# One table of steps in a new order: 31 stretches of 64-row products for 39 in a retention-and-MLP kernel

## The chip, the core and the metric

The kernel runs on one core of a Trainium2 chip. The metric is the device time of one launch in microseconds (us). Five engines work side by side, each through its own queue in order: TensorE (PE, with its weight loads shown as PEld), VectorE (DVE), ScalarE (ACT), GpSimd (POOL) and SyncE (SP), which here only issues transfers.

## What is computed

```python
# q, k, v: (8, 8, 576, 64) = batch, head, position, width; w_in 512x2048, w_out 2048x512
scores = scale * q @ k.T                      # per batch and head
ret    = scores * Dmat                        # Dmat[h, i, j] = gamma[h] ** (i - j) for i >= j, else 0
attn   = ret @ v
x = attn.transpose(0, 2, 1, 3).reshape(4608, 512)
h = x @ w_in
s = sin(alpha * h)
g = h + s * s / (alpha + 1e-9)
out = g @ w_out                               # float32
```

## The kernel before

The work is cut into nine blocks of 512 tokens: blocks 0 to 7 are the first 512 positions of one batch each, block 8 gathers the last 64 positions of all eight. Blocks pass through one pipeline: while the projections of block n run, the attention of block n+1 and the output product of block n-1 are woven in between.

*Attention.* Each batch is done in two parts p of 256 positions. `scores b p y` makes the scores of half the heads with 64x64 pieces of the PE array (16 products, line 1564), `masked` multiplies them by the decay mask on DVE (line 1576), `outer` adds up the key-value state (64-row products, line 1506), `values b p False` and `values b p True` multiply the masked scores with v (line 1606), and `add_states` adds the state of the earlier positions (line 1628); `keep` copies the result into the block's x. The state goes through `more` (two POOL operations) and `to_state`. `load` brings raw q, k and v, `cast` scales and halves them to 16 bits, and `crossed` turns them by a transfer.

*MLP.* Each of a block's 16 units is: `project` (four products of 128 rows and 512 columns, line 1745, into a PSUM bank), `sine` on ACT (line 1753), `square` on an engine that the step names (line 1762 on ACT, line 1764 on DVE or POOL), and `product` on DVE (line 1769), which writes gT and frees the bank. For blocks 0 to 2 the second matrix product is `gemm2` (four products, line 1785). Blocks 3 to 8 use a Strassen scheme instead: `weight_sum` and `row_sum` (line 1832; S1 to S4 of gT, in two parts) and seven `part_product`s of 16 products each (line 1849), read out by `after_product`.

*Order.* Everything is issued by hand from a table of 1,214 steps. A step's words say what is done, on which engine (A is ACT, V is DVE, G is POOL) and at which buffer (`@...`) or PSUM bank (op, h0, h1, h2, and m0 and m1, which are two banks each). A step issues its instructions at the end of their engines' queues. So the table alone sets each queue's order, and semaphores do the rest.

Two details matter. The two halves of `values` write the same bank by different row halves of the array. In blocks 0 to 3 PE runs dry between them:

```python
def change_rows(key):
    if key in open_turns:
        nc.tensor.drain()
        open_turns.clear()
```

`values False` puts its key into `open_turns`, and `values True` calls `change_rows`; one call empties the list for both parts. In blocks 4 to 7 `values ... False relay=G` places a mark (an empty instruction) in POOL's queue instead, and `values True` of that part waits for the mark.

Of the kernel before, what the change touches and what calls it, by code (L numbers as in the profile page):

```python
# [210 lines left out]
load 2 v 0 @raw5
load 3 k 0 @raw1
wait_for_w_out 1
load 2 v 1 @raw0
cast 2 v 1 G @v160
at.values 1 0 False m1
at.values 1 0 True
at.add_states 1 0
at.keep 1 0 V @xT1
at.next_sum 1 3  # L220
crossed 2 1 k @kT0
cast 2 v 0 G @v161
at.to_state 1 3 G
cast 2 k 0 V @k162
crossed 2 1 q @qT0
crossed 2 0 k @kT1
crossed 2 0 q @qT1
load 4 q 1 @raw2
load 3 v 0 @raw4
load 3 v 1 @raw0  # L230
load 4 v 0 @raw5
load 3 q 1 @raw3
finish 0 1
at.to_state 1 2 A
finish 0 3
at.values 1 1 True
at.add_states 1 1
gemm2 0 1 h0
gemm2 0 2 h0
at.keep 1 1 A  # L240
project 1 7 m1
project 1 6 m0
gemm2 0 3 h0
sine 1 7 @s3
# [30 lines left out]
sine 1 14 @s0  # L275
at.outer 2 (0,1) m1
at.scores 2 1 1 m0
at.evict 2 (0,1) A @kvs0
at.to_state 2 0 G @s160
cast 3 k 0 G @k163  # L280
at.more 2 1 @s321
at.more 2 2 @s320
at.to_state 2 2 G
at.more 2 3 @s321
at.to_state 2 3 G
at.to_state 2 1 G
product 1 5
gemm2 0 8 h0
gemm2 0 9 h0
square 1 9 V @ss3  # L290
product 1 9
at.masked 2 1 1 @ret0
square 1 14 A @ss0
product 1 14
sine 1 1 @s2
square 1 1 A @ss2
product 1 1
project 1 0 m1
at.scores 2 0 0 m0
project 1 4 h2  # L300
project 1 3 h1
project 1 2 op
at.masked 2 0 0 @ret1
sine 1 0 @s1
square 1 0 A @ss1
sine 1 4 @s3
square 1 4 A @ss3
sine 1 3 @s0
square 1 3 A @ss0
product 1 0  # L310
product 1 3
product 1 4
load 4 v 1 @raw1
sine 1 2 @s2
at.scores 2 0 1 m0
at.scores 2 1 0 m1
gemm2 0 10 h0
gemm2 0 11 h0
project 1 15 h1
project 1 12 h2  # L320
square 1 2 A @ss2
product 1 2
finish 0 2
gemm2 1 4 h0
gemm2 1 5 h0
at.masked 2 1 0 @ret2
sine 1 15 @s1
at.masked 2 0 1 @ret3
at.values 2 1 False m1
at.values 2 0 False m0  # L330
at.values 2 0 True
at.add_states 2 0
sine 1 12 @s3
square 1 12 V @ss1
product 1 12
cast 3 v 0 A (0) @v162
cast 3 v 0 V (1)
cast 3 v 1 A @v163
at.values 2 1 True
at.add_states 2 1  # L340
at.outer 3 (0,1) op h2
at.evict_bank 3 1 A @kvs0
at.evict_bank 3 0 A
at.more 3 1 @s320
square 1 15 V @ss0
load 4 k 0 @raw4
# [29 lines left out]
at.to_state 3 1 A
project 2 7 h2
sine 2 7 @s0
square 2 7 A @ss3
project 2 2 h0  # L380
crossed 3 0 q @qT2
project 2 1 m0
project 2 6 m1
project 2 3 op
finish 1 3
project 2 0 h1
sine 2 1 @s2
sine 2 2 @s3
square 2 2 A @ss2
product 2 7  # L390
gemm2 1 0 h2
product 2 2
# [3 lines left out]
sine 2 3 @s1
sine 2 6 @s0
square 2 1 A @ss1
product 2 1
at.scores 3 1 1 m0  # L400
square 2 6 A @ss0
sine 2 0 @s3
square 2 0 A @ss3
# [24 lines left out]
at.scores 3 0 1 m1
at.masked 3 0 1 @ret0
cast 4 k 1 G @k162  # L430
at.outer 4 (0,1) op h0
square 2 13 G @ss3
at.evict_bank 4 0 A @kvs0
at.scores 3 0 0 m0
at.masked 3 0 0 @ret2
project 2 14 h2
at.evict_bank 4 1 V
product 2 13
at.to_state 4 0 A @s160
at.more 4 1 @s321  # L440
project 2 8 op
at.values 3 1 False m1
# [47 lines left out]
load 0 v 2  # L490
load 1 v 2
make_mask_halved
project 3 0 h0
sine 3 0 @s3
square 3 0 A @ss2
weight_sum T3 0 V
product 3 0
gemm2 2 0 op
cast 5 v 0 G @v162
cast 5 k 1 G @k160  # L500
load 0 k 2
load 1 k 2
cast 5 q 1 G @q161
project 3 1 h1
sine 3 1 @s2
project 3 2 h2
sine 3 2 @s0
# [24 lines left out]
product 3 1
cast 5 v 1 G @v163
square 3 6 A @ss0
gemm2 2 6 op
project 3 7 h1
at.scores 4 1 0 m1
sine 3 7 @s1
product 3 6
cast 0 v 2 G  # L540
at.masked 4 1 0 @ret1
square 3 7 A @ss1
# [1488 lines left out]
```

## Time and profile before

| | us |
|---|---|
| median of three runs | 298.53 |
| lowest and highest | 297.3 and 298.81 |
| the profiled execution, whole | 297.56 |
| its span, first to last instruction | 295.8 |
| busy in it: PE, DVE, ACT, POOL | 284.9, 223.8, 218.1, 141.0 |
| DMA: moved, mean rate | 49.95 MB, 169 GB/s |

PE is the longest queue by 60 us. A row of the chain of waits names the start, the length and the work that ended last there; the same row as "PE ... x16" means that PE's own queue was the last thing waited for. Busy times of PE are modelled from starts, so small gaps are better read from the chain.

### The profile page before, as it was taken

To read this page: it belongs to the slowest core of one execution; us is meant where nothing else is said; L and a number is where in the kernel's file an instruction comes from. 1 tells how busy PE (TensorE), PEld (TensorE's weight loads), DVE (VectorE), ACT (ScalarE), POOL (GpSimd) and SP (SyncE) were. 2 spreads that over 40 slices of the span, in tenths; PEclk is the share of its full clock that TensorE was granted. 3 is DMA by queue.
4 is the path that set the end of the run, shared out by engine and by line. 5 is a ranking of instruction groups with operands and counts; after the bars stand their busy time and mean duration, and the time that the engine had idled before them with its cause. 6 is when DMAs were issued, how large, how long until landed. Compare 5 with 4: busy or idle time off the path is not lost.

```text
span 295.8 us, 8407 instructions
## 1 busy us (share of the span) xinstructions
PE 284.9 (96%) x3480; PEld 182.6 (62%) x3480; DVE 223.8 (76%) x316; ACT 218.1 (74%) x361; POOL 141.0 (48%) x151
## 2 busy tenths in 40 slices
PE   6789999999999999999999999999999999999993
PEld 4566545555545544455666666666776677676883
DVE  2596977788349776889988798869868785877863
ACT  2578935997595897977878896798679878888500
POOL 5684678565688685736439933956232000000000
PEclk9999999999999999999999999999999999999999
DMA  7999999998998999978899985984423101200124
GB/s 216 347 234 210 243 282 320 253 256 217 244 225 184 174 164 229 250 148 204 164 239 163 251 180 145 232 151 120 88 77 104 38 2 38 73 15 23 53 73 124
DMA packets 121767, 49.95 MB, mean 169 GB/s; under 512 B 78721, under 2 KB 119681, under 8 KB 121729
## 3 DMA queue, kind: packets, MB, share of 16 engines
q1 hardware_dynamic: 117920, 44.78, 63.5%
q0 software_dynamic: 2688, 4.19, 7.8%
q8 instruction: 27, 0.44, 0.6%
q10 hardware_dynamic: 1120, 0.44, 0.6%
q14 instruction: 12, 0.09, 0.1%
HBM read 36.75 MB, written 9.44 MB: 156 GB/s over the span
## 4 chain that ended last, share of the span: by engine, by line
PE 82%; DMA 9%; DVE 3%; ACT 2%; POOL 1%; SPq 1%; issue 1%; ACTq 0%; POOLq 0%
PE hps L1745 40%; PE hps L1849 23%; PE ops L1785 12%; DMA raw<-in_v_dram 3%; DMA w_in<-in_moe_w_in_dram 3%; PE o L1606 3%; PE sc L1564 2%; DMA raw<-in_k_dram 2%; DVE S L1832 1%; PE kv L1506 1%; DVE gT L1769 1%; PE o L1628 1%; SPq L1350 1%; POOL k L1396 1%; ACT s L1753 1%
## 5 line engine op out<-in xcount | busy, mean ns | idle before, releaser
L1769 DVE SCALAR_TENSOR_TENSOR gT<-ss,inva,hps 128x512 f16<-128x512 f16 x144 | 103.7, 743 | 36.0 <-ACT ss L1762 32.5
L1745 PE MATMUL hps<-xT,w_in 128*128 128x512 f16 (+1 forms) x532 | 120.2, 372 | 0.6 <-DMA w_in<-in_moe_w_in_dram 0.6
L1753 ACT ACTIVATE s<-hps,alpha_t 128x512 f16<-128x512 f32 x144 | 96.1, 683 | 30.4 <-PE hps L1745 29.5
L1745 PEld LDWEIGHTS <-w_in 128*128 128x128 f16 x596 | 65.6, 114 | 51.4 <-DMA w_in<-in_moe_w_in_dram 0.9
L1762 ACT ACTIVATE ss<-s 128x512 f16<-128x512 f16 x125 | 76.9, 629 | 5.9 <-DVE gT L1769 3.3
L1785 PE MATMUL ops<-w_out,gT 128*128 128x512 f16 x192 | 46.0, 380 | 0.0
L1849 PEld LDWEIGHTS <-gT 128*128 128x128 f16 x384 | 37.3, 98 | 7.5
L1396 POOL TENSOR_TENSOR k<-raw,cn 128x1024 f16<-128x1024 f32 (+1 forms) x17 | 29.5, 1736 | 20.9 <-DMA raw<-in_k_dram 18.4
L1849 PEld LDWEIGHTS <-S 128*128 128x128 f16 x288 | 28.1, 98 | 6.1
L1785 PEld LDWEIGHTS <-gT 128*128 128x128 f16 x192 | 17.9, 98 | 20.3
L1396 POOL TENSOR_TENSOR q<-raw,cn 128x1024 f16<-128x1024 f32 x13 | 25.1, 1937 | 3.7 <-PE o L1606 2.4
L1849 PE MATMUL hps<-T,gT 128*128 128x256 f16 x192 | 22.8, 273 | 0.0
L1849 PE MATMUL hps<-w_out,S 128*128 128x256 f16 x192 | 22.8, 273 | 0.0
L1849 PE MATMUL hps<-w_out,gT 128*128 128x256 f16 x192 | 22.8, 273 | 0.0
L1551 POOL TENSOR_TENSOR s<-kvs,cn 128x256 f32<-128x256 f32 x21 | 13.8, 659 | 16.3 <-ACT kvs L1320 8.8
L1322 POOL CAST v<-raw 128x1024 f16<-128x1024 f32 x10 | 10.3, 1037 | 21.8 <-DMA raw<-in_v_dram 20.0
L1576 DVE TENSOR_TENSOR ret<-sc,mask 128x1024 f16<-128x1024 f32 x16 | 19.2, 1219 | 1.6 <-PE sc L1564 1.6
L1552 POOL TENSOR_TENSOR kvs<-s,kvs 128x256 f32<-128x256 f32 x21 | 17.5, 833 | 3.9 <-DVE kvs L1322 1.2
L1576 DVE TENSOR_TENSOR ret<-sc,mask_halved 128x768 f16<-128x768 f32 x16 | 15.1, 954 | 3.7 <-PE sc L1564 3.6
L1320 ACT CAST xT<-o 128x1024 f16<-128x1024 f32 (+1 forms) x15 | 16.2, 1122 | 1.9 <-PE o L1628 1.9
L1832 DVE TENSOR_TENSOR S<-gT,S 128x1024 f16<-128x1024 f16 x24 | 17.4, 730 | 0.1
L1745 PE MATMUL hps<-xS,w_in 128*128 128x512 f16 x64 | 14.8, 379 | 0.0
(78 smaller groups left out, 265.6 us busy)
## 6 DMA issues: line engine op xcount, KB each, us to landing
raw<-in_q_dram SPq DMA_DIRECT2D x16, 512.0 KB, 5.3
out_dram<-osb SPq DMA_DIRECT2D x32, 256.0 KB, 2.9
raw<-in_k_dram SPq DMA_DIRECT2D x8, 512.0 KB, 6.1
raw<-in_v_dram SPq DMA_DIRECT2D x8, 512.0 KB, 6.3
raw<-in_v_dram SPq DMA_DIRECT2D x32, 128.0 KB, 3.5
raw<-in_k_dram SPq DMA_DIRECT2D x32, 128.0 KB, 3.7
w_in<-in_moe_w_in_dram POOLq DMA_DIRECT2D x4, 512.0 KB, 11.9
w_out<-in_moe_w_out_dram POOLq DMA_DIRECT2D x4, 512.0 KB, 13.2
```

What stands on the lines that cost most here:

```text
L1320: eng.copy(d_, s_)
L1396: eng.tensor_tensor(dst[:, a0:a1].rearrange("p a r t d -> p t (a r) d"), t_.rearrange("p (t a) x -> p t a x", t=2)[:, :, a0:a1].rearrange( ...
L1551: nc.gpsimd.tensor_tensor(s32, self.kvs[:, c - 1], g1.unsqueeze(2).to_broadcast([P, 4, D]), MULT)
L1552: nc.gpsimd.tensor_tensor(self.kvs[:, c], s32, self.kvs[:, c], ADD)
L1576: nc.vector.tensor_tensor(ret.rearrange("p t (z x) -> p (t z) x", z=2)[:, :, 0:n], sc.rearrange("p t (z x) -> p (t z) x", z=2)[:, :, 0:n], ...
L1745: matmul(hps_of[n, fc][0][:, cols], w_in16[fc // 4][:, a, fc % 4 :: 4], xs[n][:, a, cols], start=(a == 0 and part != 1), stop=(a == KT - 1 ...
L1753: nc.scalar.activation(s_t, hps, mybir.ActivationFunctionType.Sin, bias=0.0, scale=alpha_t[:, fc : fc + 1],)
L1762: nc.scalar.activation(ss_t, s_t, mybir.ActivationFunctionType.Square)
L1769: nc.vector.scalar_tensor_tensor(gT[n][:, fc, :], ss_t, inva[:, fc : fc + 1], hps, MULT, ADD)
L1785: matmul(ops[n, c, cols.start][:, cols], gT[n][:, fk, c * P : (c + 1) * P], w_out16[:, fk, cols], start=(fk == 0), stop=(fk == FC - 1), sk ...
L1832: made = eng.tensor_tensor(out_, x, y, op)
L1849: matmul(acc[:, 256 * j : 256 * j + 256], lhs[:, x, 128 * j : 128 * j + 128], rhs[:, x], start=(tag is not None and j == js[0] and p == 0 ...
```

## The change

The table keeps its 1,214 steps and every function; the multiset of matrix products, transfers and results is the same. From row 133 on, in block 0's last units, nearly every step has another place, and some have another engine, bank or buffer. A stretch is a run of 64-row products with no 128-row product between; there are 39 before and 31 after. Counted over the whole table, squares go from 125 on ACT, 11 on DVE and 8 on POOL to 84, 43 and 17; row sums from 48 on DVE to 28 on DVE and 20 on POOL; casts of q and k from 38 on POOL and 6 on DVE to 29 and 15; casts of v from 14 on POOL, 6 on ACT and 1 on DVE to 9, 10 and 2. Two lines of the difference:

```diff
-row_sum 4 S3 0 V
+row_sum 4 S3 0 G
...
-square 7 0 A @ss1
+square 7 0 V @ss1
```

PE, at block 4's first scores. `sc` is the PSUM tile of one `scores` step, `kT` and `qT` the turned keys and queries, `ops` a `gemm2` result. Before:

```order
L1564 MATMUL sc_2116<-qT0_205,kT1_259 64x64
L1564 LDWEIGHTS kT1_259
L1564 MATMUL sc_2116<-qT0_205,kT1_259 64x64
L1785 LDWEIGHTS gT_1584
L1785 MATMUL ops_2135<-w_out16_74,gT_1584 128x512
```

After, at the same block's first scores:

```order
L1564 MATMUL sc_2123<-qT2_344,kT1_259 64x64
L1564 LDWEIGHTS kT1_259
L1564 MATMUL sc_2123<-qT2_344,kT1_259 64x64
L1564 LDWEIGHTS kT3_1211
L1564 MATMUL sc_2140<-qT1_271,kT3_1211 64x128
```

A second group of 16 now follows the first at once, where a `gemm2` unit stood.

POOL, around the marks of block 5's `values`. The marks are empty and have no row: before, the second one stands between the rows of `vs16` and `q162`; after, both stand between the rows of `gT_2516` and `s320`. `vs16`, `k163` and `q162` are casts, `ss2` is a square, `gT_2516` a row sum, `kvs0` the state. Before:

```order
L1544 TENSOR_TENSOR s160_279<-kvs0_246,cn_67 128x256
L1544 TENSOR_TENSOR sS_75<-kvs0_246,cn_67 128x256 [waits Pool_49]
L1322 CAST vs16_2899<-vs32_2277 128x512
L1396 TENSOR_TENSOR q162_287<-raw1_123,cn_67 128x2x8x64 [waits PE_49]
L1551 TENSOR_TENSOR s321_776<-kvs0_246,cn_67 128x256 [waits Activation_49]
```

After:

```order
L1396 TENSOR_TENSOR k163_894<-raw0_121,cn_67 128x2x8x64 [waits DMAHW5_49,DMAHW6_49,DMAHW4_49,PE_49]
L1764 TENSOR_TENSOR ss2_541<-s1_523 128x512 [waits DVE_49,Activation_49]
L1396 TENSOR_TENSOR q162_287<-raw1_123,cn_67 128x2x8x64
L1832 TENSOR_TENSOR gT_2516<-gT_2516 128x4x256 [waits PE_49]
L1551 TENSOR_TENSOR s320_623<-kvs0_246,cn_67 128x256 [waits PE_49,Activation_49]
```

Ahead of the marks POOL now has two casts of 128x1024, a square and a row sum; before, two state operations and a small cast stood there.

DVE, in the second half of block 7. `gT` rows of line 1769 are `product`s, `S` and `gT<-gT` rows of line 1832 are row sums, `osb` a result. Before:

```order
L1769 SCALAR_TENSOR_TENSOR gT_4110<-ss2_541,inva_69,hps_4537 128x512
L1895 TENSOR_TENSOR osb_4595<-hps_4578,low_4157 128x512
L1769 SCALAR_TENSOR_TENSOR gT_4598<-ss1_539,inva_69,hps_4599 128x512
L1832 TENSOR_TENSOR gT_4110<-gT_4110 128x4x256
L1832 TENSOR_TENSOR S2_1_2582<-gT_4110 128x1024
L1832 TENSOR_TENSOR S1_1_2606<-gT_4110,S2_1_2582 128x1024
L1832 TENSOR_TENSOR S4_1_2776<-gT_4110,S2_1_2582 128x1024
```

After:

```order
L1769 SCALAR_TENSOR_TENSOR gT_4104<-ss1_539,inva_69,hps_4550 128x512
L1769 SCALAR_TENSOR_TENSOR gT_4104<-ss3_563,inva_69,hps_4557 128x512
L1769 SCALAR_TENSOR_TENSOR gT_4104<-ss1_539,inva_69,hps_4569 128x512
L1764 TENSOR_TENSOR ss0_525<-s2_537 128x512
L1895 TENSOR_TENSOR osb_4611<-hps_4586,low_4168 128x512
L1764 TENSOR_TENSOR ss3_563<-s3_550 128x512
L1832 TENSOR_TENSOR gT_4104<-gT_4104 128x4x256
```

Squares have come into DVE's queue, and of the four row sums of the second part one is left there.

More of the change, by code (lines that the diff above doesn't have):

```diff
@@ L218 @@
+cast 2 q 1 V @q160
+at.add_states 1 1
 at.add_states 1 0
 at.keep 1 0 V @xT1
-at.next_sum 1 3
-crossed 2 1 k @kT0
-cast 2 v 0 G @v161
[L223 to L244, printed above, removed]
@@ L272 @@
+square 1 7 V @ss2
+product 1 7
+cast 2 v 0 G @v161
+product 1 10
+square 1 5 G @ss1
+product 1 5
 sine 1 9 @s3
@@ L280 @@
+sine 1 0 @s2
+product 1 1
+project 1 3 h1
+load 3 v 0 @raw2
+sine 1 3 @s1
+square 1 3 A @ss0
+product 1 9
+load 3 v 1 @raw3
+load 4 v 0 @raw5
+square 1 0 A @ss2
+project 1 2 op
 cast 3 k 0 G @k163
-at.more 2 1 @s321
-at.more 2 2 @s320
+at.scores 2 0 0 m0
+gemm2 0 10 h0
+at.masked 2 0 0 @ret1
 at.to_state 2 2 G
[L284 to L309, printed above, removed]
 product 1 0
 product 1 3
-product 1 4
[L313 to L323, printed above, removed]
+sine 1 2 @s3
+square 1 2 A @ss3
@@ L324 @@
+cast 3 v 0 G (0) @v162
+project 1 4 h2
+sine 1 4 @s2
+square 1 4 A @ss2
+product 1 2
+gemm2 0 11 h0
+finish 0 2
+at.scores 2 1 0 m1
+at.scores 2 0 1 m0
+at.masked 2 0 1 @ret3
+project 1 15 h1
+load 3 q 0 @raw4
+load 0 v 2
+product 1 4
+project 1 12 op
+sine 1 12 @s1
+square 1 12 A @ss3
 gemm2 1 4 h0
+cast 3 v 1 A @v163
+at.masked 2 1 0 @ret2
+product 1 12
 gemm2 1 5 h0
-at.masked 2 1 0 @ret2
-sine 1 15 @s1
-at.masked 2 0 1 @ret3
+at.to_state 2 1 G
 at.values 2 1 False m1
+at.values 2 1 True
 at.values 2 0 False m0
@@ L331 @@
 at.values 2 0 True
-at.add_states 2 0
[L333 to L339, printed above, removed]
+cast 3 v 0 G (1)
+load 3 q 1 @raw3
+sine 1 15 @s2
+square 1 15 A @ss0
+at.outer 3 (0,1) op h2
+at.to_state 2 3 V
+at.add_states 2 0
 at.add_states 2 1
-at.outer 3 (0,1) op h2
+load 4 v 1 @raw0
+product 1 15
+cast 4 q 1 G @q160
 at.evict_bank 3 1 A @kvs0
[L343 to L346, printed above, removed]
@@ L376 @@
[L376 to L392, printed above, removed]
+load 4 k 0 @raw2
+cast 4 k 0 G (0) @k163
+sine 2 3 @s3
+product 2 6
 gemm2 1 8 h0
 gemm2 1 9 h0
-gemm2 1 10 h0
[L396 to L403, printed above, removed]
@@ L424 @@
-square 2 9 A @ss0
-product 2 9
-sine 2 13 @s3
 finish 1 0
+at.scores 3 0 0 m0
+load 5 q 1 @raw2
+load 1 v 2
+product 2 13
+at.masked 3 0 0 @ret2
 at.scores 3 0 1 m1
 at.masked 3 0 1 @ret0
[L430 to L435, printed above, removed]
-project 2 14 h2
[L437 to L442, printed above, removed]
+load 0 k 2
+at.outer 4 (0,1) h0 h1
+at.evict_bank 4 0 V @kvs0
@@ L490 @@
[L490 to L507, printed above, removed]
+project 3 2 h2
+sine 3 2 @s2
+square 3 0 V @ss0
+product 3 0
+project 3 1 h1
+sine 3 1 @s1
+project 3 4 m1
+sine 3 4 @s0
+product 2 12
+load 5 k 1 @raw4
+square 3 1 G @ss1
+cast 5 k 0 V @k162
+at.more 4 3 @s321
+square 3 2 A @ss3
@@ L532 @@
[L532 to L542, printed above, removed]
+crossed 5 0 k @kT2
+project 3 6 h2
+cast 0 v 2 G
+project 3 9 h0
+load 5 v 1 @raw5
+product 3 1
+at.scores 4 0 0 m0
+at.scores 4 1 0 m1
+sine 3 6 @s2
+gemm2 2 4 op
+load 6 v 0 @raw2
+project 3 7 h1
+at.to_state 4 3 G
+load 5 q 0 @raw0
+square 3 6 A @ss3
+gemm2 2 5 op
+at.masked 4 1 0 @ret1
+product 3 6
+load 3 v 2
@@ L576 @@
+sine 3 10 @s2
+square 3 10 V @ss2
+weight_sum T2 0 V
+at.to_state 4 2 A
 cast 0 k 2 G
+gemm2 2 8 op
 gemm2 2 9 op
 gemm2 2 10 op
-sine 3 12 @s0
-square 3 12 A @ss1
-product 3 12
-at.values 4 1 False m1 relay=G
-square 3 8 A @ss3
+gemm2 2 11 op
+product 3 10
+square 3 11 A @ss3
+product 3 11
+sine 3 8 @s2
+cast 5 q 0 V @q162
+at.values 4 0 False m0 relay=G
+finish 2 2
+at.values 4 1 False m1 relay=G
+cast 0 q 2 G
+at.outer 5 (0,1) h0 h2
+at.values 4 0 True
+at.values 4 1 True
+load 2 k 2
+square 3 8 A @ss0
@@ L706 @@
-square 4 10 A @ss1
-part_product 3 5 op
+product 3 14
+gemm2 2 15 op
+weight_sum T1 0 V
+project 4 5 h1
+square 3 13 A @ss2
+sine 4 2 @s3
+product 3 13
+at.more 5 2 @s321
+square 4 2 A @ss1
+cast 2 v 2 G
+product 4 0
+sine 4 5 @s2
+part_product 3 1 op
+project 4 7 m1
+weight_sum T4 0 V
+finish 2 3
+square 4 5 A @ss2
+cast 6 v 0 A @v160
+product 4 2
+product 4 5
+at.more 5 3 @s321
+at.scores 5 0 1 m0
+sine 4 7 @s3
+load 6 k 0 @raw4
+weight_sum T1 1 V
+row_sum 3 S2 1 V
+cast 6 k 0 G @k161
+project 4 1 h0
@@ new lines @@
+square 4 7 A @ss1
+weight_sum T2 1 V
+after_product 3 1
+project 4 3 h2
+part_product 3 2 - first=1
+product 4 7
+at.masked 5 0 1 @ret2
+load 6 q 1 @raw2
+at.scores 5 1 0 m1
+at.to_state 5 1 V
+sine 4 3 @s0
+square 4 3 A @ss2
+at.scores 5 0 0 m0
+row_sum 3 S1 1 V
+after_product 3 2
+project 4 4 h1
+row_sum 3 S4 1 V told_to=G
+at.masked 5 0 0 @ret3
+product 4 3
+sine 4 4 @s2
+part_product 3 6 op
+after_product 3 6
+at.masked 5 1 0 @ret1
+load 6 v 1 @raw4
+project 4 9 m0
+sine 4 1 @s3
+square 4 1 A @ss3
@@ new lines @@
+project 4 6 h2
+at.to_state 5 3
+square 4 4 A @ss2
+product 4 4
+product 4 1
+sine 4 9 @s0
+square 4 9 A @ss1
+product 4 9
+sine 4 6 @s0
+square 4 6 A @ss2
+product 4 6
+part_product 3 7 - first=6
+row_sum 3 S1 0 V
+project 4 10 h1
+at.to_state 5 2 G
+after_product 3 7
+project 4 8 h0
+load 3 k 2
+project 4 12 h2
+part_product 3 5 op
+at.scores 5 1 1 m0
+load 2 q 2
+load 3 q 2
+weight_sum T4 1 V
+cast 6 k 1 G @k163
+load 7 v 1 @raw0
+sine 4 10 @s1
+crossed 6 0 k @kT2
+sine 4 12 @s3
+cast 6 v 1 A @v161
@@ L774 @@
-square 5 1 A @ss1
-product 4 15
-project 5 2 m0
-sine 5 2 @s1
-project 5 6 h0
-square 5 2 A @ss3
+cast 2 k 2 V
+load 4 k 2
+crossed 2 2 k
+at.evict_bank 6 0 A @kvs0
+after_product 3 3
+square 4 11 V @ss2
+at.evict_bank 6 1 V
+at.more 6 1 @s320
+load 7 k 0 @raw1
+crossed 6 0 q @qT2
+product 4 11
+at.keep 5 0 A @xT0
+at.values 5 1 True
+at.add_states 5 1
+at.keep 5 1 A
+project 4 14 op
+sine 4 14 @s2
+row_sum 4 S2 0 V
+row_sum 4 S4 0 G
+at.more 6 2 @s321
+row_sum 4 S1 0 G
+square 4 14 A @ss3
+product 4 14
@@ new lines @@
+part_product 3 4 h0
+after_product 3 4
+project 4 13 h2
+sine 4 13 @s1
+at.more 6 3 @s320
+project 5 2 m1
+at.to_state 6 0 @s160
+project 5 0 m0
+load 5 k 2
+crossed 6 1 k @kT3
+project 4 15 h0
+cast 6 q 1 V @q160
+crossed 6 1 q @qT3
+part_product 4 1 op
+sine 5 0 @s3
+load 7 v 0 @raw2
+square 5 0 V @ss1
+square 4 13 A @ss0
+product 4 13
+product 5 0
+load 4 v 2
+load 5 v 2
+cast 7 v 0 G @v162
+project 5 3 h1
+sine 4 15 @s3
+square 4 15 A @ss2
+product 4 15
+after_product 4 1
+row_sum 4 S3 1 V
@@ L807 @@
+product 5 9
+at.scores 6 1 1 m0
+product 5 6
+square 5 4 A @ss0
+part_product 4 7 - first=6
+project 5 12 h1
+sine 5 12 @s2
+at.masked 6 1 0 @ret1
+row_sum 5 S3 0 G
+project 5 8 h0
+product 5 4
+after_product 4 7
+at.to_state 6 3
+row_sum 4 S1 1 V
+at.to_state 6 1
+project 5 7 h2
+project 5 5 m1
+part_product 4 5 op
+at.masked 6 1 1 @ret3
+sine 5 8 @s0
+square 5 8 A @ss3
+sine 5 7 @s0
+cast 7 q 0 G @q160
+square 5 12 A @ss2
+load 7 k 1 @raw1
+product 5 8
 cast 7 k 1 G @k163
-square 5 4 A @ss3
-product 5 4
@@ new lines @@
+crossed 4 2 k
+after_product 5 1
+part_product 5 2 - first=1
+row_sum 5 S2 1 V
+project 6 4 h1
+at.more 7 1 @s320
+at.masked 7 0 1 @ret2
+at.scores 7 1 0 m0
+square 6 1 G @ss2
+crossed 2 2 q
+product 6 1
+at.scores 7 1 1 m1
+after_product 5 2
+sine 6 4 @s2
+sine 6 2 @s1
+row_sum 5 S4 1 V told_to=G
+cast 6 v 2 G
+square 6 4 V @ss1
+product 6 4
+square 6 2 A @ss0
+product 6 2
+project 6 11 h2
+at.masked 7 1 1 @ret3
+project 6 5 h0
+project 6 7 h1
+cast 4 v 2 A
+at.masked 7 1 0 @ret1
+part_product 5 6 op
```

1302 lines of the change are left out of this document (582 added, 720 removed).

## The prediction

> **What bounds the kernel now.** I read the page's busy times, then the chain of waits, then the busy times by stage, then the groups by line.
>
> ```profile
> span 295.8 us, 8407 instructions
> PE 284.9 (96%) x3480; PEld 182.6 (62%) x3480; DVE 223.8 (76%) x316; ACT 218.1 (74%) x361; POOL 141.0 (48%) x151
> PEclk9999999999999999999999999999999999999999
> ```
>
> PE is busy 96% at full granted clock; the next queue, DVE, is at 76%. So PE's list is the floor, and the question is how much shorter it gets and whether the others still feed it. The chain, in order of time:
>
> ```profile
> 33.63 10.15 DMA raw<-in_v_dram
> 43.80 1.05 ACT v L1320
> 44.90 0.45 PE kv L1506 x32
> ...
> 60.25 0.64 PE kv L1506 x64
> ...
> 72.80 0.57 PE o L1606 x32
> 73.47 0.42 PE o L1606 x16
> ...
> 116.35 0.86 PE hps L1745 x4
> 117.22 0.47 PE sc L1564 x32
> 117.69 0.99 PE hps L1745 x4
> ...
> 122.99 0.30 PE sc L1564 x16
> 123.29 0.97 PE ops L1785 x4
> ...
> 291.42 0.42 DVE osb L1895
> ```
>
> Three things are to be seen. First, PE stands still for a transfer until 44.90: block 1's second v lands at 43.78, ACT casts it, and only then do the key-value products start. Secondly, a stretch of 64-row products has a fixed price: four 128-row products take 0.86 after their like but 0.99 or 0.97 right after a stretch, and 16 products alone take 0.30 where 32 take 0.47. Thirdly, in the 64-row work at 72.80 something takes time inside the stretch: that is the emptying of PE between the two halves of `values`. By stage:
>
> ```profile
> core 0: us, PE busy (x) PEld busy (x) DVE busy (x) ACT busy (x) POOL busy (x), PEclk, DMA share, GB/s
> 45.00:136.00 91.00, 90.71 (x1193) 47.89 (x1192) 67.86 (x91) 73.65 (x129) 61.19 (x62) 1.00 0.97 220
> 136.00:163.00 27.00, 27.00 (x374) 18.40 (x373) 24.02 (x31) 21.34 (x35) 16.08 (x16) 1.00 0.96 191
> 163.00:198.00 35.00, 34.93 (x434) 24.58 (x432) 28.54 (x39) 28.86 (x46) 21.68 (x21) 1.00 0.84 194
> 198.00:241.00 43.00, 43.00 (x493) 29.03 (x491) 34.79 (x49) 34.89 (x56) 12.06 (x14) 1.00 0.30 80
> 241.00:291.00 50.00, 49.90 (x472) 37.51 (x471) 37.27 (x58) 31.36 (x52) 0.61 (x1) 1.00 0.14 45
> ```
>
> From 45 to 291 PE lacks 0.29 + 0 + 0.07 + 0 + 0.10 = 0.46 us of its time. That is all the waiting that a better order could still take away there. DVE is fullest from 136 to 163: 24.02 of 27.
>
> **The change, part by part.** The prices of work that changes its engine:
>
> ```profile
> L1764 DVE TENSOR_TENSOR ss<-s x11: 416/419/1884, 24.1 to 100.0; 128x512 f16<-128x512 f16 x11
> L1764 POOL TENSOR_TENSOR ss<-s x8: 1041/1041/1044, 28.0 to 105.2; 128x512 f16<-128x512 f16 x8
> L1762 ACT ACTIVATE ss<-s 128x512 f16<-128x512 f16 x125 | 76.9, 629 | 5.9 <-DVE gT L1769 3.3
> L1396 DVE TENSOR_TENSOR q<-raw,cn 128x1024 f16<-128x1024 f32 x2 | 2.9, 1446 | 2.8 <-DMA raw<-in_q_dram 2.8
> L1396 POOL TENSOR_TENSOR q<-raw,cn 128x1024 f16<-128x1024 f32 x13 | 25.1, 1937 | 3.7 <-PE o L1606 2.4 <-DMA qT<-q 0.9 <-DMA raw<-in_q_dram 0.2
> L1322 POOL CAST v<-raw 128x1024 f16<-128x1024 f32 x10 | 10.3, 1037 | 21.8 <-DMA raw<-in_v_dram 20.0 <-PE hps L1745 1.9
> L1769 DVE SCALAR_TENSOR_TENSOR gT<-ss,inva,hps 128x512 f16<-128x512 f16 x144 | 103.7, 743 | 36.0 <-ACT ss L1762 32.5 <-POOL ss L1764 2.6
> L1822 DVE TENSOR_TENSOR T<-w_out 128x1024 f16<-128x1024 f16 x2 | 1.4, 688 | 0.0
> L1822 DVE TENSOR_TENSOR T<-T,w_out 128x1024 f16<-128x1024 f16 x2 | 3.4, 1688 | 0.0
> L1322 DVE COPY kvs<-kv 128x512 f32<-128x512 f32 x1 | 0.7, 681 | 0.0
> L1544 DVE TENSOR_TENSOR s<-kvs,cn 128x256 f16<-128x256 f32 x1 | 0.4, 424 | 0.0
> ```
>
> And row sums and squares on DVE, first between 45 and 240 with POOL at work, then from 245 on, when POOL has stopped:
>
> ```profile
> L1832 DVE TENSOR_TENSOR S<-gT,S 128x1024 f16<-128x1024 f16 x14 | 10.7, 761 | 0.1
> L1832 DVE TENSOR_TENSOR S<-gT 128x1024 f16<-128x1024 f16 x8 | 7.7, 956 | 0.3 <-issue 0.2
> L1832 DVE TENSOR_TENSOR gT<-gT 128x1024 f16<-128x1024 f16 x8 | 7.4, 935 | 0.0
> L1764 DVE TENSOR_TENSOR ss<-s 128x512 f16<-128x512 f16 x8 | 4.7, 603 | 0.6 <-ACT s L1753 0.6
> ...
> L1832 DVE TENSOR_TENSOR S<-gT,S 128x1024 f16<-128x1024 f16 x8 | 5.3, 686 | 0.1
> L1832 DVE TENSOR_TENSOR S<-gT 128x1024 f16<-128x1024 f16 x4 | 2.8, 690 | 0.1
> ```
>
> *Stretches.* Two lone groups of 16 cost 2 x (0.30 + 0.97 - 0.86) = 0.82, one group of 32 costs 0.47 + 0.99 - 0.86 = 0.60. A merged stretch thus saves 0.22. Of the eight that go, one goes ahead of the key-value products at 44.90 (block 1's second scores now run straight into them). They wait for the v cast in either order: the load of that v stands at the same place in SP's queue, behind the same three transfers, and its buffer is long free. So this one is worth nothing, and seven count: 7 x 0.22 = 1.54 less.
>
> *Emptying of PE.* Before, blocks 1, 2 and 3 issue both `values False` ahead of the first `values True`, so each pays once. After, block 1 does so, but blocks 2 and 3 issue False, True, False, True and pay twice: two more. Price: from 72.80 to 73.47 32 products take 0.67 where 32 elsewhere take 0.47, and the next 16 take 0.42 instead of 0.30: 0.2 to 0.3; I take 0.3, both differences: 2 x 0.3 = 0.6 more.
>
> *The old waits.* At best all 0.46 goes, at worst nothing: I take 0.2 less.
>
> *DVE.* Squares +32 at 0.42 = 13.4; row sums -20 at 0.86 (25.8 us for 30 beside POOL) or 0.69 (alone), say 0.79 = -15.8; seven full and two half casts of q and k at 1.45 and half of it = +11.6; bank copies, states, v casts and results that came from ACT and POOL, about +9. In all +18: 242 of 296 us, 82%. ACT loses 41 squares at 0.63 (-26). POOL gets nine squares (+9.4) and 20 row sums, of which before has none on POOL. Bounds: twice the 128x512 square (2.08), and the cast of q, equal in elements (1.94); I take the cast as the nearest, so +39. It gives away seven full casts (-13.6), two half ones (-2), and v casts and states (-10): 164 us, 55%. No engine passes PE over the run, so it matters where it is dense.
>
> The densest place is block 3, between its first and its last part product (136.7 to 164.5 before):
>
> ```profile
> 136.70:164.50 27.80, 27.80 (x384) 19.44 (x383) 24.17 (x32) 22.23 (x36) 16.88 (x17) 1.00 0.97 193
> ```
>
> There PE gets three projections less (3 x 0.86): 25.2. DVE gets one product less (-0.74), and a weight sum (0.69 to 1.69, say 1.1), a half cast (0.7), a square (0.42), a bank copy (0.68) and a state (0.42) more: 26.7. So DVE falls behind by up to 1.5 us in that stretch. The banks hold some of it (PE may run ahead by a few units, at 0.86 each), so PE loses 0 to 1.5; I take 0.8. From 198 to 241 DVE has 34.79 of 43; eight us are to spare, and I add nothing there.
>
> *POOL's marks.* In block 5 the marks stand behind a square, a cast and a row sum, and a cast ahead of these whose load went long before. The square waits for the sine of block 4's unit 10. From that unit's projection to the marks PE has three projections, two part products and two groups of 16: 3 x 0.86 + 2 x 1.72 + 0.43 = 6.5 (a part product's 16 products have half the columns of a projection's four: twice 0.86). Sine, square, cast and row sum take about 0.7 + 1.04 + 1.94 + 1.94 = 5.6. Margin 0.9, and POOL is held up by DVE as DVE is by POOL. Late by 0 to 1.94; I take 0.1. In blocks 4 and 6 a key-value group of 64 products (0.64 at 60.25) stands behind the marks' `False`, which covers their way; in block 7 and in the last 64 positions only one group of 16 does (0.30 at most): 0 to 0.2 each, counted in the range.
>
> *SP and the loads.* Block 2's loads have a new order, and each waits for another cast. Its last q load goes when ACT has cast block 1's v (44.85):
>
> ```profile
> raw<-in_q_dram SPq DMA_DIRECT2D x16, 512.0 KB, 5.3
> ```
>
> It lands at 50.2; POOL then has three casts of k and q, two of v and one square before block 2's key-value products: 3 x 1.94 + 3 x 1.04 = 8.9, so 59.1, for products that started at 60.25. Margin 1.1: I take 0, with 0.5 in the range. The end is the same: the last two half products, a 0.42 result and its store.
>
> *Sum.* -1.54 + 0.6 - 0.2 + 0.8 + 0.1 = -0.24. Against the profiled execution (297.56) that is 297.3; against the median, which lies 0.97 above it, 298.3. Work that can be late in small amounts in thirty places is not in this sum, and in a fuller DVE it adds rather than takes: I put 0.2 for it and say **298.5**.
>
> **Where DVE and POOL meet.** Beside POOL a row sum takes 25.8 us for 30, 0.86 each, and alone 0.69; a square 0.60 on the mean instead of 0.42. So such an instruction pays 0.17 to 0.18 for POOL's company. The change makes POOL's instructions longer and puts more of these on DVE: 32 more squares x 0.18 = 5.8 us over the run, and the tail, where POOL was silent, gets POOL work too.
>
> The Trainium skill (SBUF — State Buffer, "Who interferes with whom") says that a DVE instruction with two inputs in SBUF contends with a GpSimd instruction that reads SBUF, and that the later one blocks until the first is done. The trace agrees: 419 ns at the median and 1884 at most for the same square. By that rule alone, a square that comes behind a POOL row sum waits its whole 1.94, and two such waits in dense places make the 301.6 of the third rival below; without it the sum stays at 298.5.
>
> **Rivals.** *PE's emptying is free and all waits go* (ends faster): -1.54 - 0.46 = 296.5. For it: the old order left only 0.46. Against it: the row at 73.47. *A mark is late* by one POOL instruction in block 5: 298.5 - 0.1 + 1.94 = 300.3. For it: the margin of 0.9. Against: the three operations take only what their rows say. *DVE becomes the bound* (ends slower): where DVE's stretch passes PE's, each blocked square or row sum (1.88 for the longest square's 0.42, above) goes straight to PE. It decides from the point at which DVE's 26.7 in block 3 gets above 25.2 by more than the banks hold; with one POOL row sum (1.94) lost in block 3 and one more in block 4 or 5 instead of the 0.8: 298.5 - 0.8 + 3.9 = 301.6. For it: 26.7 over 25.2 and the rows just quoted. Against: PE waited only 0.46 us in a run with DVE at 24.02 of 27.
>
> **How the numbers follow.** The forecast has 0.5, with a range of its own from 297.1 (no new wait and none of the old: 298.53 - 1.54 + 0.6 - 0.46) to 300.0 (DVE's whole 1.5, 0.5 for the loads and 0.4 for the marks: 298.53 - 0.94 + 2.4). Free emptying has 0.14, a late mark 0.09, DVE as the bound 0.27. A change below 0.5% (1.5 us) can hardly be told from none. Faster needs below 297.0, which only the first rival and a little of the forecast reach: 0.16. Slower needs above 300.0: DVE's case, half of the marks', a little of the forecast: 0.34. Same: 0.5. The range goes from 297.0 to 302.0: some 0.1 is left out on either side.
>
> **What would show it.** 31 stretches; row prices of 0.30 and 0.47 as before; key-value products of block 1 at 44.9 again; five gaps of 0.3 inside `values` instead of three. If DVE is the bound, PE's busy time between block 3's first and last part product falls short of the stretch by 1 us or more and the chain passes through DVE lines there. If a mark is late, the chain goes through POOL ahead of line 1606. I am wrong on the faster side if block 1's products start before 44, since I hold that wait fixed.

## Result: 0.7% slower, and the profile after

The changed kernel takes 300.13 us at the median of 20 runs (298.53 to 303.14), the kernel before 297.85 on the same chip (20 runs). The ratio of the times is 1.0071, 95% interval [1.0047, 1.0096]: slower, by some 2.1 us. Ratios and intervals leave out the runs that are more than 1.5% above the fastest of their kernel; medians are of all runs. The profiled execution of the changed kernel is a late one, 302.99 with a span of 301.3, so its 5.5 us over the span before (295.8) are more than the usual run loses. From its page:

```profile
span 301.3 us, 8420 instructions
PE 286.1 (95%) x3480; PEld 183.4 (61%) x3480; DVE 243.3 (81%) x350; ACT 194.2 (64%) x317; POOL 169.5 (56%) x161
PEclk9999999997999999999999999999999999999999
```

The loads of the engines are close to what the prediction worked out (DVE 242, POOL 164). The clock row has a 7 in one slice, which was a 9 before. By stage, busy time of PE, PEld, DVE, ACT and POOL, then the clock:

```profile
45.00:136.00 91.00, 87.83 (x1171) 45.95 (x1163) 74.36 (x104) 65.03 (x114) 52.12 (x55) 0.98 1.00 226
136.00:163.00 27.00, 27.00 (x228) 17.39 (x227) 24.16 (x35) 22.17 (x35) 16.24 (x15) 1.00 0.65 157
163.00:198.00 35.00, 33.75 (x556) 23.69 (x557) 29.97 (x41) 25.04 (x40) 25.73 (x21) 1.00 0.88 189
198.00:241.00 43.00, 42.97 (x501) 29.99 (x493) 39.42 (x54) 27.05 (x43) 27.51 (x26) 1.00 0.42 92
241.00:291.00 50.00, 49.85 (x473) 36.07 (x472) 41.40 (x66) 25.35 (x41) 22.62 (x12) 1.00 0.11 38
```

PE lacks 3.17 us in the first of these stages and 1.25 in the third; before it lacked 0.29 and 0.07. The stage from 136 to 163, where I had expected DVE to hold PE up, has no gap at all. PE's waits from 45 to 291 (us in total, times, longest), before:

```profile
PE kv L1506 <- ACT v L1320: 0.3, 1, 0.3
```

and after:

```profile
PE sc L1564 <- DMA qT<-q: 2.0, 1, 2.0
PE hps L1745 <- DVE gT L1769: 1.2, 2, 0.7
PE kv L1506 <- ACT v L1320: 0.5, 1, 0.5
PE hps L1745 <- ACT xT L1320: 0.3, 1, 0.3
PE sc L1564 <- DMA kT<-k: 0.2, 1, 0.2
PE hps L1745 <- DVE xT L1322: 0.2, 1, 0.2
```

*The late turn.* The chain of waits of the changed kernel around the first of these:

```profile
61.73 5.92 DMA qT<-q
67.66 0.14 issue
67.79 0.42 PE sc L1564 x16
68.21 1.82 PE ops L1785 x4
70.03 1.69 PE hps L1745 x4
71.72 0.86 PE ops L1785 x4
```

The scores wait for block 2's last turned q. After the wait four products of 512 columns take 1.82 and 1.69 instead of 0.86: PE runs at half rate, 1.7 us more in all. SP's queue shows that the turn goes out late. Before, the four turns go out one right behind the other:

```profile
52.66 2.92 SPq L1418 DMA_TRANSPOSE kT<-k  x1
55.68 1.33 SPq L1418 DMA_TRANSPOSE qT<-q  x1
57.10 1.26 SPq L1418 DMA_TRANSPOSE kT<-k  x1
58.46 1.25 SPq L1418 DMA_TRANSPOSE qT<-q  x1
```

After, the first takes 6.13 us, right behind three loads and two stores (what holds it there the trace doesn't settle), and a store and a load of block 4 stand between the turns:

```profile
50.59 6.13 SPq L1418 DMA_TRANSPOSE qT<-q  x1
56.81 0.53 SPq L1778 DMA_DIRECT2D out_dram<-osb  x1
57.43 1.30 SPq L1418 DMA_TRANSPOSE kT<-k  x1
58.79 0.57 SPq L1350 DMA_DIRECT2D raw<-in_q_dram  x1
59.46 2.19 SPq L1418 DMA_TRANSPOSE kT<-k  x1
61.73 1.73 SPq L1418 DMA_TRANSPOSE qT<-q  x1
```

*The blocked square.* PE's 1.2 us for gT (1.57 by the starts of its products) are at 174 to 176. DVE's and POOL's rows there:

```profile
172.36 2.34 DVE L1764 TENSOR_TENSOR ss<-s 128x512 f16<-128x512 f16 x1
171.31 3.10 POOL L1832 TENSOR_TENSOR S<-gT,S 128x1024 f16<-128x1024 f16 x1
```

A square that takes 0.42 alone takes 2.34 and ends 0.3 after a POOL row sum that began 1 us ahead of it. The Trainium skill (SBUF — State Buffer, "Who interferes with whom") says that a DVE instruction with two inputs in SBUF contends with a POOL instruction that reads SBUF; the trace agrees. All squares of the run on DVE, with the shortest, the median and the longest in ns:

```profile
L1764 DVE TENSOR_TENSOR ss<-s x43: 410/424/2336, 24.0 to 281.4; 128x512 f16<-128x512 f16 x43
```

Seven others took 0.9 to 1.4 us, each beside a POOL instruction, but none of these is followed by a wait of PE above 0.3.

*The lost cover.* Block 2's x is copied by DVE and ACT in turns (second number: length):

```profile
79.28 0.73 DVE L1322 CAST xT<-o 128x512 f16<-128x512 f32 x1
81.41 0.74 DVE L1322 CAST xT<-o 128x512 f16<-128x512 f32 x1 [1.40 <-ACT xT L1320]
```

Before, PE had 24 products to do between the attention of block 2 and its first projection; after, it has 8 (1.9 us), and its products there start 0.45 and 0.34 late. The row before:

```profile
74.91 5.35 PE L1785 MATMUL ops<-w_out,gT 128*128 128x512 f16 x24
```

**Where the 5.5 us went.** I took the distance from each PE product's start to the next, less the usual one for its kind, over all 3,480 rows after 30 us. At the borders of the stretches it sums to 7.27 us before and 5.42 after: the eight stretches gave 1.85, or 0.23 each. Single delays of over 0.1 us sum to 2.29 before and 9.98 after: the late turns 2.13 and 0.42, the half rate 1.7, the square 1.57, the copies of x 0.79, two more emptyings 0.6, and smaller ones. 7.7 less 1.85 is 5.8, near the 5.5 of the spans. Below, "delays" is this second sum.

### The profile page after: what moved, and what is told of

It reads as the page before. It is cut to its first block, busy times and chain, and to the rows that moved or that the text cites. A ratio compares the mean times of both kernels' runs of the same rounds, so it can differ in the third digit from the quotient of the medians.

```text
span 301.3 us, 8420 instructions
## 1 busy us (share of the span) xinstructions
PE 286.1 (95%) x3480; PEld 183.4 (61%) x3480; DVE 243.3 (81%) x350; ACT 194.2 (64%) x317; POOL 169.5 (56%) x161
## 4 chain that ended last, share of the span: by engine, by line
PE 71%; DMA 10%; DVE 6%; ACT 5%; SPq 3%; POOL 2%; issue 1%; DVEq 0%; ACTq 0%
PE hps L1745 31%; PE hps L1849 22%; PE ops L1785 12%; DMA w_out<-in_moe_w_out_dram 5%; SPq L1350 2%; PE sc L1564 2%; DMA qT<-q 2%; PE o L1606 2%; DMA raw<-in_q_dram 2%; DVE ss L1764 2%; DVE gT L1769 2%; ACT s L1753 2%; ACT ss L1762 1%; POOL q L1396 1%; ACT xT L1320 1%
## 5 line engine op out<-in xcount | busy, mean ns | idle before, releaser
L1762 ACT ACTIVATE ss<-s 128x512 f16<-128x512 f16 x84 | 52.1, 628 | 4.6 <-DVE gT L1769 2.7
L1785 PE MATMUL ops<-w_out,gT 128*128 128x512 f16 x192 | 46.8, 385 | 0.2 <-DMA w_out<-in_moe_w_out_dram 0.2
L1396 POOL TENSOR_TENSOR k<-raw,cn 128x1024 f16<-128x1024 f32 (+1 forms) x15 | 25.0, 1673 | 22.9 <-DMA raw<-in_k_dram 22.8
L1764 POOL TENSOR_TENSOR ss<-s 128x512 f16<-128x512 f16 x17 | 19.3, 1139 | 25.8 <-ACT s L1753 20.2
L1832 POOL TENSOR_TENSOR S<-gT,S 128x1024 f16<-128x1024 f16 x12 | 26.8, 2250 | 9.6 <-DVE S L1832 6.4
L1764 DVE TENSOR_TENSOR ss<-s 128x512 f16<-128x512 f16 x43 | 24.8, 581 | 6.1 <-ACT s L1753 5.6
L1396 POOL TENSOR_TENSOR q<-raw,cn 128x1024 f16<-128x1024 f32 x8 | 15.7, 1956 | 6.0 <-DMA raw<-in_q_dram 5.8
L1552 POOL TENSOR_TENSOR kvs<-s,kvs 128x256 f32<-128x256 f32 x21 | 16.7, 795 | 3.8 <-DVE kvs L1322 2.1
L1320 ACT CAST xT<-o 128x1024 f16<-128x1024 f32 (+1 forms) x13 | 14.0, 1099 | 3.2 <-PE o L1628 2.9
```

What stands on the lines that cost most here:

```text
L1320: eng.copy(d_, s_)
L1396: eng.tensor_tensor(dst[:, a0:a1].rearrange("p a r t d -> p t (a r) d"), t_.rearrange("p (t a) x -> p t a x", t=2)[:, :, a0:a1].rearrange( ...
L1552: nc.gpsimd.tensor_tensor(self.kvs[:, c], s32, self.kvs[:, c], ADD)
L1762: nc.scalar.activation(ss_t, s_t, mybir.ActivationFunctionType.Square)
L1764: eng.tensor_tensor(ss_t, s_t, s_t, MULT)
L1785: matmul(ops[n, c, cols.start][:, cols], gT[n][:, fk, c * P : (c + 1) * P], w_out16[:, fk, cols], start=(fk == 0), stop=(fk == FC - 1), sk ...
```

## The experiments

Each kernel ran in the same session as the kernel before; all ratios are to it, with 95% intervals.

**1. The late turn.**

```diff
 crossed 2 1 k @kT1
+crossed 2 0 k @kT2
+crossed 2 0 q @qT2
...
 load 4 q 1 @raw1
-crossed 2 0 k @kT2
...
-crossed 2 0 q @qT2
```

> The changed kernel with two steps moved: the turns of block 2's first k and q stand right behind the turn of its second k, ahead of a 512 KB load that is needed two blocks later. Theory A (block 2's last turned q is late in SP's queue): the wait of 2.1 us ahead of block 2's third group of scores falls under 0.4, and PE's clock row shows no dip in that slice; the time falls from 300.1 by 2.1, or by 4.4 if the dip (eleven 512-column products at 0.43 instead of 0.22) belongs to most runs: 295.7 to 298.0, ratio to the kernel before 0.993 to 1.000. Theory B (DVE and POOL block each other, and the extra emptyings cost the rest): the wait goes, but the time stays within 0.5 of 300.1, ratio 1.006 or more.

Ratio 1.008 [1.0044, 1.0115]. In the profiled run the wait at 65 and the dip of the clock are gone, delays are 5.57 and the span is 297.4; but this run (299.19) is the fastest of twelve, and the median did not fall (300.61). So this wait, at the size that the first profile showed it, is not what the usual run loses; the other traces have 0.1 to 0.75 at 60 to 66, and other late transfers at 88 and 99. This trace has none of these, and its span is still 1.6 us above the span before: its delays are 3.3 more (the square 1.63, the copies of x 0.85, two emptyings 0.6, the wait at 44 0.27), against the 1.85 of the stretches.

**2. Two emptyings.**

```diff
 at.values 2 1 False m1
-at.values 2 1 True
 at.values 2 0 False m0
+at.values 2 1 True
```

(and the like in block 3)

> The changed kernel with one step moved in each of blocks 2 and 3: both first halves of values stand ahead of both second halves, as in the kernel before, so PE runs dry once per block. Theory of the prediction: two gaps of 0.3 us go, 300.1 becomes 299.5, ratio to the kernel before 1.005. Rival (emptying PE costs nothing, since what follows waits for results anyway): 300.1, ratio 1.007.

Ratio 1.009 [1.0056, 1.0123]: not the 1.005, though the trace has three gaps of 0.31 inside `values` instead of five. Delays are 11.06: this profiled run, a late one at 303.78, had waits of 0.55 for a turned q at 66, 0.58 at 88 and 1.7 for a cast of k at 99. If the 0.6 is there, it is below what varies from run to run.

**3. The blocked square.**

```diff
-square 5 0 V @ss1
+square 5 0 A @ss1
```

> The changed kernel with one square, that of block 5's first unit, on ACT instead of DVE. Theory B (a DVE square that meets a POOL row sum is blocked until the other ends): the 2.34 us square of 172.4 goes, and the 0.87 and 0.70 us of PE's waiting at 174.3 and 176.1 with it: 298.5 in every run that has the meeting, ratio 1.002. Theory A: the meeting belongs to the profiled run or is made good later; 299.8 to 300.1, ratio 1.006 to 1.007.

Ratio 1.0055 [1.0015, 1.0095]. The waits at 174 and 176 are gone, and these have come between 160 and 210, where the changed kernel had none at these lines:

```profile
PE kv L1506 <- POOL k L1396: 1.2, 1, 1.2
PE hps L1849 <- DVE gT L1769: 0.8, 1, 0.8
```

PE comes earlier to block 7's key-value products and finds POOL still casting k. It looks as if the wait had moved, but that isn't shown: the trace of 2, where the square is still on DVE, has 0.67 and 0.95 at the same two places besides.

**4. All three together.**

> The three edits of the other runs together. If the three costs add up: 300.1 - 2.1 - 0.6 - 1.6 = 295.8, ratio to the kernel before 0.993; 293.5 (0.985) if PE's clock dip of 2.3 us belongs to most runs of the changed kernel. If another wait takes their place: above 298, ratio 1.000 or more.

Ratio 0.9999 [0.9961, 1.0038], delays 9.23. The medians, 299.49 against 298.48, give 1.0034. So the three together are worth 1.1 us by the medians and 2.1 by the ratios, where their sum was 4.3. The rest is in waits at 77 (1.10), 88 (1.16), 99 (0.64) and 201 (0.94), as far as this one trace shows.

**5. All POOL row sums on DVE** (20 steps from `G` to `V`, on top of 4).

> The kernel with the three edits, and all 20 row sums of POOL on DVE instead. Theory C (POOL is packed with row sums of 2.1 us, so its casts of k come late for the key-value products near 195, DVE is blocked near 200, and PE then waits for a product at 203): the waits at 195 (0.2 to 1.4), 203 (0.9) and at POOL's marks and sums near 241 to 247 (0.1 to 0.2 each) go; POOL falls from 170 to about 128 us, DVE rises by 20 x 0.69 less what contention it loses, to about 250; time 1.0 to 2.0 below that of the three edits, ratio to the kernel before 0.993 to 0.997. Rival D (DVE is the bound once it has them): new waits for products in blocks 4 to 7, time 1 to 3 above that of the three edits, ratio 1.003 to 1.010. The front half up to 160 us should not change.

Ratio 1.011 [1.0079, 1.0142]. POOL falls to 125.7, DVE rises to 248.8, and delays fall to 7.17 in the profiled run (its time, 299.84, is the lowest of six), but the median rises by 1%. The waits that 4 had at 195 (for POOL) and 203 are gone; seven others of 0.2 to 0.7 have come at 119, 161, 168, 196, 214, 267 and 288, five of them for DVE by the profile (it names nothing for those at 161 and 267). My theory C falls: the waits that it named went, but the time did not follow, and rival D, that DVE has no room for all of them, comes nearest.

**6. The front mended** (on top of 4).

```diff
-load 4 q 1 @raw1
+load 3 q 1 @raw1
...
-load 3 q 1 @raw3
+load 4 q 1 @raw3
...
-at.keep 2 0 V A @xT0
-at.keep 2 1 A V
+at.keep 2 0 V @xT0
+at.keep 2 1 A
...
```

> The kernel with the three edits, and two places of the front mended. First, block 2's x is copied as in block 1: one part whole on DVE, the other whole on ACT, where now each engine copies half of each part and they take turns. Second, the load of block 3's second q takes the place (and buffer) of the load of block 4's second q ahead of it, the two casts change places, its turn goes right behind that of k, and block 4's second k load goes behind the first. Theory E (the front half's waits come from what the new order puts first in SP's queue and from the lost cover of four gemm2 units behind block 2's state products): the gaps at 77 to 79 (1.1 and 0.33) fall to 0.3 in sum, the wait for a turned q at 88 (0.6 to 1.2) and the wait for a cast of k at 99 (0.6 to 1.7) go under 0.3; time 2 to 3 below the three edits, ratio to the kernel before 0.990 to 0.994. Rival F (the transfers as a whole arrive too late, whatever their order, since the 16 DMA engines are full up to 105 us): another transfer is waited for instead, time within 0.7 of the three edits, ratio 0.998 to 1.002.

Ratio 1.0058 [1.0031, 1.0085], slower than both forecasts. The copies of x cost nothing any more and the waits at 88 and 99 are gone, as theory E had it, but the time did not follow. DVE and PE show now:

```profile
89.18 1.23 DVE L1396 TENSOR_TENSOR q<-raw,cn 128x1024 f16<-128x1024 f32 x1 [1.11 <-DMA raw<-in_q_dram]
90.33 2.35 DVE L1576 TENSOR_TENSOR ret<-sc,mask 128x1024 f16<-128x1024 f32 x2
```

```profile
92.73 1.02 PE L1745 MATMUL hps<-xT,w_in 128*128 128x512 f16 x4 [0.62 <-DVE ret L1576]
94.93 1.02 PE L1745 MATMUL hps<-xT,w_in 128*128 128x512 f16 x4 [1.18 <-DVE gT L1769]
```

DVE stands in the cast of block 4's q, whose load is late, with masks and products queued behind it. In the trace of 4 PE waited for the turned q meanwhile (until 89.7); with that gone it meets this. 5 and 6 together:

> The edits of the other two runs together: three edits, block 2's copies, block 3's q, and all row sums on DVE. If theories C and E hold: 3 to 5 below the three edits, ratio to the kernel before 0.983 to 0.991. If C alone or E alone holds: as that run. If D and F hold: above 1.003.

Ratio 1.0147 [1.0122, 1.0173]. The same cast now cost PE 1.95 and 1.18, and half rate after them.

**7. The back.** On top of 4:

```diff
-row_sum 4 S4 1 G told_to=G
+row_sum 4 S4 1 V told_to=G
...
-at.keep 6 1 V
+at.keep 6 1 A
```

> The kernel with the three edits, and two letters changed in block 4 and 6: the row sum S4 (second part) of block 4 goes from POOL to DVE, and the copy of block 6's second part of x from DVE to ACT. Theory G (once the meeting of square and row sum at 172 is gone, PE comes 1.6 us earlier to block 7's key-value products and finds POOL's chain of row sum, cast, load and cast behind; the wait moved there): the row sum of 2.1 us leaves that chain, the waits at 195 (0.2 to 1.4) and 203 (0.94 and 0.26) fall under 0.4 in sum; time 1 to 2 below the three edits, ratio to the kernel before 0.993 to 0.997. Rival D (DVE has no room for the row sum, as with all 20): a wait for DVE of 0.5 or more between 180 and 215 takes their place, ratio 0.999 to 1.003.

Ratio 1.004 [1.0005, 1.0075], above both forecasts. Block 7's key-value products no longer wait, but PE waits 1.03 for ACT's second copy of x at 197 and 0.80 for DVE at 176. With the front, and DVE's casts of block 4's q put behind the products and masks that had stood behind them:

> As the run before, and the front mended as tried already (block 2's x copied by one engine for each part, block 3's q loaded and turned earlier), but with DVE's two casts of block 4's q behind the products that stood behind them in its queue. Theory H (in the first try the wait only moved: DVE stood in a cast whose load was late, 1.1 to 2.2 us, with masks and products behind it): no wait of PE above 0.6 between 76 and 100, where the three edits had 1.1, 0.33, 0.38, 1.16 and 0.64; with the back part the ratio to the kernel before is 0.984 to 0.992. Rival F (the transfers are late in any order): another wait of 1 us or more up to 105, ratio 0.994 to 1.000.

Ratio 1.0024 [0.999, 1.0058], delays 6.79: above what theory H and rival F forecast. The longest wait between 76 and 100 is 0.66 now. The waits left:

```profile
PE hps L1745 <- ACT xT L1320: 0.9, 1, 0.9
PE hps L1745 <- DVE gT L1769: 0.5, 1, 0.5
PE sc L1564 <- DVE gT L1769: 0.5, 1, 0.5
PE kv L1506 <- DVE gT L1769: 0.4, 1, 0.4
PE o L1606 <- DVE gT L1769: 0.4, 1, 0.4
```

**8. The price of a stretch** (on top of 4, seven stretches split; one of the seven):

```diff
 at.scores 2 1 0 m1
+project 1 15 h1
 at.scores 2 0 1 m0
...
-project 1 15 h1
```

> The kernel with the three edits, with seven of its merged stretches of 64-row products split again: one group of 128-row products is moved between two groups of 16 scores, in blocks 2 to 6; the work is the same. Theory of the prediction (each stretch costs 0.22 of PE's time): the fixed cost at the borders of the stretches grows by 7 x 0.22 = 1.5 and the time by as much, ratio to the kernel before 1.005. Rival (borders cost nothing once PE waits for others anyway): ratio as with the three edits, 1.000.

Ratio 1.0118 [1.0071, 1.0165], 3.5 us above the kernel of 4 by the ratios (2.7 by the medians). The borders cost 6.62 instead of 5.32: 1.30 for seven, 0.19 each, which bears out the price of a border; the time rose by more than that. The rest is in waits at 126 (1.0) and 182 (1.2 and 0.4) that the other traces don't have. Ahead of the first, DVE has a square of 1.92 us beside a POOL cast (122.73). The second lasts until two masks are done on DVE (181.91 to 183.73), which now start only 2 us ahead of the next scores. Whether the first belongs to the split or to this one run isn't shown.

**9. Order and engines apart.** The order of the changed kernel with the old engine for each of the 109 steps whose engine had changed, and the other way round:

> The changed order with the kernel before's choice of engine for every step: 53 squares, 20 row sums, 18 casts, 7 bank copies, 7 states, 2 sums and 2 copies of x go back to the engine they had; the order of the 1,214 steps, banks and buffers are those of the changed kernel. Theory J (the new engines are what takes the slack: POOL's row sums of 2.1 us, DVE's squares that meet them): PE's waits in blocks 4 to 8 fall to the 0.5 us of the kernel before, only the front's 1 to 3 us and the two emptyings stay; the stretches give 1.8: 297.0 to 299.0, ratio to the kernel before 0.997 to 1.003. Theory K (the new order itself leaves the steps too little cover, whatever engine does them): waits of 5 us or more as with the changed engines, ratio 1.005 to 1.010. Theory L (order and engines belong together: in the new order the old engines are late in other places): ratio above 1.012.

> The kernel before with the changed kernel's choice of engine for the same 109 steps; its order, banks and buffers are as before, with 39 stretches and three emptyings. Theory J: PE's waits rise from 2 us to 5 or more, DVE at 243 and POOL at 170 us: ratio 1.010 to 1.018. Theory K: the waits stay under 3.5: ratio 0.999 to 1.005. Theory L: ratio above 1.018.

Ratios 1.077 [1.0715, 1.0824] and 1.23 [1.2236, 1.2363]. Engine rows and clock of the second:

```profile
PE 299.5 (82%) x3480; PEld 186.2 (51%) x3480; DVE 252.5 (69%) x350; ACT 194.7 (53%) x317; POOL 169.3 (46%) x161
PEclk9999999679669999899899999689699999999998
```

The sums of ACT and POOL are those of the changed kernel, DVE has 9 us more and PE 13 (its half rate, below, is in them), and yet the time is 67 us longer: single waits of 10, 14 and 9 us stand in it. Both ratios are in theory L's range: neither half is good or bad by itself, and I read it so that a step's engine is chosen for the queue it joins. Totals by engine don't show this.

**10. Five more places**, found in the trace of the second kernel of 7:

```diff
-cast 4 q 0 V @q161
...
 at.evict_bank 4 0 V @kvs0
+cast 4 q 0 V @q161
...
-weight_sum T2 0 V
...
 product 3 11
+weight_sum T2 0 V
...
-row_sum 4 S4 1 V told_to=G
...
 product 5 2
+row_sum 4 S4 1 V told_to=G
...
-at.keep 6 1 A
+at.keep 6 1 V
...
-cast 7 q 1 V @q162
+cast 7 q 1 G @q162
```

> The kernel with the three edits and the mended front, and five more places: DVE's cast of block 4's first q goes behind the masks of block 3 (its load was late, 1.9 us, with two products behind it), a weight sum of block 3 behind two products, block 4's row sum S4 (second part) on DVE behind three products, and block 7's second q cast on POOL; the copy of block 6's second part of x is on DVE again. Theory M (the changed order holds its 1.8 us of fewer borders, and what outweighs them is a number of single places that can be mended one by one): the waits of over 0.1 us, 6.8 in the run before this one, fall under 4.5, ratio to the kernel before 0.990 to 0.996. Theory N (there is too little slack left: what is taken away at one place comes back at another): waits of 6 or more, ratio 1.000 to 1.005.

Ratio 0.9962 [0.9936, 0.9987], 296.89 against 298.25: faster than both kernels. Its delays are 4.7, and both figures are just outside those of theory M (4.5 and 0.996) and far from theory N's. PE's waits from 45 to 291:

```profile
PE hps L1745 <- DVE gT L1769: 0.7, 1, 0.7
PE kv L1506 <- ACT v L1320: 0.5, 1, 0.5
PE kv L1506 <- issue: 0.3, 1, 0.3
```

So with its 31 stretches and nearly all of its engines kept, the new order is 1.1 us faster than the old one once single places in it are mended: they are what outweighed its gain. Which of these places is worth how much isn't shown, neither of the five nor of the ones before, since a single edit mostly let another wait come up.

## Why the prediction was wrong, point by point

- *Stretches, -1.54:* right. The borders gave 1.85 for eight; the one ahead of the key-value products at 44 was worth nothing, as said, since the wait there grew from 0.47 to 0.74. The split gave 0.19 each, against 0.22.
- *Emptyings, +0.6:* right in the trace, five gaps of 0.30 to 0.33. Taking two away (experiment 2) did not show in the time.
- *SP and the loads, 0, with 0.5 in the range:* this is the step that failed. I followed block 2's loads through POOL's casts to the key-value products, and these were on time (60.03). But the same queue carries the turns, which the scores need; I did not go on to them, nor count what stands between them. In the profiled run it cost 2.5 us of waiting and 1.7 us of half rate. In the traces of 2, 3, 4, 8 and the first kernel of 7, PE stands 1.3 to 2.8 us between 60 and 101 for turned q and k and for casts of k (which wait for their load in 3, 4 and 8); in that of 1, the fastest of its twelve runs, not at all. What it costs the usual run stays open: turning block 2's k and q earlier left the median where it was, and the trace of 1 has 3.3 us more delays than before without any late transfer.
- *What is late in small amounts, 0.2, and the old waits, -0.2:* mis-sized. Nine other traces of the same order, with a few steps mended, have delays of 5.6 to 11.1 where before had 2.3, so 3.3 us more at the least, where the two terms put nothing. One term was plainly left out: block 2's first projections lost the cover of 16 products, 0.7 to 1.8 us for the copies of x in the traces that don't mend it.
- *DVE, +0.8 in block 3:* no wait there. The mechanism of the third rival, a blocked square, held PE up once, in block 5's first unit, for 1.57 us. I looked for the stage that was fullest on the mean; what counts is where a row sum of POOL meets a short DVE step that PE waits for.
- *POOL row sums at 1.94:* twelve of the twenty took 2.25 on the mean (26.8 us), 2.13 at the median, and the others were like them. So they lay above both bounds, 1.94 and 2.08, and the lower was taken.

```profile
L1832 POOL TENSOR_TENSOR S<-gT,S x12: 2113/2126/3102, 167.9 to 288.1; 128x1024 f16<-128x1024 f16 x12
```

- *Marks, 0.1:* right. Nothing in block 5, 0.14 and 0.21 in block 7 and the end.

The prediction gave slower 0.34; its likeliest case was a sum near nothing, where the kernel lost 2.1 us, because the gains were all counted from rows and most of the losses from margins that I had followed to one reader only. That the measured 300.13 lies next to the 300.3 of the late mark is luck: no mark was late in block 5.

## What to carry to other kernels

When a written-out order is changed, follow each moved transfer to every step that reads its result, and go through its queue for what now stands ahead. Take a wait away, and look in the next trace for the engine that was hidden behind it; here one such place mostly replaced another, and only with some dozen mended did the time fall below the old one. Do not judge an exchange of engines by busy totals: with ACT and POOL within 1 us and DVE within 11 (241.6 and 252.5), the kernels of 10 and of 9 took 297 and 367 us.

## What the runs showed of the hardware

PE's rate falls to half after a wait that is shorter than I had thought. In all the traces together, from 30 us on, waits of 2.13, 2.9, 3.7, 3.8 and 5.7 to 14 us were each followed by products at half rate for 2 to 5 us, 1.0 to 2.1 us lost; so was a pair of 1.95 and 1.18 within 3 us. One of 2.01 was not, and none of the 70 or so from 0.6 to 1.75. An example from the second kernel of 9, eight products in 3.57 us instead of 1.9:

```profile
73.53 3.57 PE L1785 MATMUL ops<-w_out,gT 128*128 128x512 f16 x8 [9.84 <-DVE gT L1769]
```

The Trainium skill (TensorE: Matmul & The Clock Gate, "Part 1: The HAM clock gate") gives an idle window of about 3.4 us for the fall; here some 2 us were enough. The wait of 2.13 cost nearly twice itself, with the 1.7 us of half rate behind it.
